# Turned squares with the place in the quarter outermost, and their copies three steps later

## The chip, the cores and the metric

The kernel runs on one core of a Trainium2 chip. The metric is the time of the whole kernel on the device in microseconds (us); lower is better. Times before and after are medians of several runs; a profile is one further execution that the hardware profiler recorded.

## What is computed

Two layers follow one another. The first is a gated attention without softmax: the scores of a sequence with itself are symmetric, the negative ones are cut off, and the rest is squared. The second sends each of the 19,968 resulting rows through one of eight small networks, chosen by a hash of its token.

```python
B, S, D = 8, 2496, 256          # z has 64 columns
scores = (1.0 / S) * np.matmul(z, z.transpose(0, 2, 1))
attn = np.maximum(scores, 0.0) ** 2
x = (u * np.matmul(attn, v)).reshape(B * S, D)

expert_idx = token_ids * np.int64(2654435761) % 8
for e in range(8):              # w1: 256 x 1024, w2: 1024 x 256
    mask = expert_idx == e
    out[mask] = np.maximum(x[mask] @ w1[e], 0.0) @ w2[e]
```

All values are 32-bit floats.

## The kernel before

**Tiles and groups.** A sequence has 2496 positions: 19 tiles of 128 and one of 64 (tile number `TM` = 19). Four tiles make a group, so a batch has `NG` = 5 groups g = 0 to 4; the last has 448 positions, the others 512. The kernel goes through the 8 batches b, and in each through its groups: `for n, (b, g) in enumerate(groups)`. A group's positions are the queries, columns of the matmuls. For each group it sums, over all 20 tiles t of keys, `v[t]` times the squared scores of tile t with the group. The sum stands in two PSUM tiles `acc`, one for each half of the 256 columns of v.

**Half of the scores are never computed.** As scores are symmetric, `scores(b, g)` (line 203) computes only the key tiles from the group's own on; these squares are called fresh and lie in tiles `made[b, g, key group]`, 128 partitions by 4 key tiles by 512 queries, from the pool `apool` of six rooms. TensorE writes a score tile to PSUM (line 210, six buffers, `mm_ps`), ScalarE writes its ReLU to the room (line 218; for g = 0 VectorE takes every eighth, line 216), and later ScalarE squares it in place (line 226). What lies on the other side of the diagonal is obtained by turning: a room of 4 by 4 tiles is transposed into a `mirror` tile, which a later group reads. Seven mirror tiles exist (one serves the routing's sorting at first, `sorting`, and in the expert stage their room holds weights).

**How a room is turned.** VectorE's transpose works on squares of 32 by 32. `turns_of` (line 234) does a room in four turns c, one for each quarter of 32 columns: VectorE transposes the quarter's squares into a buffer `stage` of 128 partitions by 512 elements (line 241, pool `spool`, five buffers). The four quarters r of the stage's partitions must then go to partitions c of the mirror: three of them by DMA from SBUF to SBUF, issued by SyncE (line 251), and the fourth, which stays on its partitions, by a copy on ScalarE (line 249). The mirror's layout is (partition, i, r, s, q): query tile i, place r of the query in its tile's quarters, key tile s, and q in the quarter. So a row of 512 elements of the stage is broken into four pieces of 128 elements (512 bytes), or three where the last group's fourth tile has no such quarter. Rooms on the diagonal are completed in place by small transposes on VectorE (`own_turns`, line 262).

**The order of the work** is written out by hand (`order = tc.manual_schedule()`, line 569): each engine's instructions stand in its queue as the program emits them, and an engine takes them in that order. A step of the attend loop (lines 664 to 691) emits two matmuls, the halves of one key tile (`attend`, line 319), then two squares, then turns, 1.2 a step on average (`turn_scores`, line 280), then `between` (line 595), which counts the steps in `i` and also places the routing's small work. `turn_scores` first emits the copies of the turns of the step before (`to_copy`). `turn_now` forces what a reader still lacks. At a step of t = 8 the group's u is loaded (`load_u`); for g = 1, 2, 3, 4 parts of the next batch's v are loaded too, at g = 3 the next batch's z. All of these, like the mirrors' transfers, are issued by SyncE. After the loop `attend_last` (line 326) takes the half tile 19, then the next group's scores are emitted, then the last three key tiles (`LATE`), half after half, each followed by `gate`.

**Leaving the group.** `gate` (line 334) transposes acc on VectorE into `x_q` (line 339, pool `qpool`, two buffers), writes it to DRAM (`x_way`, four DMAs, line 346) so that quarters and columns change places, and three steps later reads it back as rows (`fetch`, lines 349 and 351, one DMA or, for the last group, two). GpSimd multiplies by u and places each row at the slot of its expert. The columns of acc stand in the order of the queries: tile i outside, then r, then q. `squares` (line 308) gives the matmul its columns: fresh squares are contiguous there, mirrors are read in runs of 32.

From about 1560 us on the second layer runs: for blocks of rows of one expert, two chains of matmuls (lines 742 and 754).

Of the kernel before, what the change touches and what calls it, by code (L numbers as in the profile page):

```python
# [10 lines left out]
F32 = mybir.dt.float32  # L11
# [13 lines left out]
def kernel(  # L25
# [10 lines left out]
    nc = tc.nc  # L36

    B, S, D = u.shape
    K = z.shape[-1]
    N = B * S  # L40
    E, _, F = moe_w1.shape
# [15 lines left out]
    NQ = P // Q  # L57
# [11 lines left out]
    def pool(name, bufs, **kw):  # L69
        return ctx.enter_context(tc.tile_pool(name=name, bufs=bufs, **kw))  # L70
# [8 lines left out]
    NA = NG + 1  # L79
    apool = pool("apool", NA)  # L80
    xpool = pool("xpool", 3)
    qpool = pool("qpool", 2)
    spool = pool("spool", 5)

    x_dram = nc.dram_tensor("x_rows", (NS * P, D), F32)

    x_way = [nc.dram_tensor(f"x_way_{k}", (G, NQ, Q, D), F32) for k in range(2)]


    slot_dram = nc.dram_tensor("slot_tokens", (P * NS,), I32)
# [30 lines left out]
    zn, zT, v_sb, u_sb, x_q, made, mirror, to_square, to_turn, to_fetch, gated = {}, {}, {}, {}, {}, {}, {}, [], [], [], []  # L123
# [110 lines left out]
    def turns_of(b, a, g):  # L234

        key = b, a, g
        def turn(c):
            if key not in mirror:
                mirror[key] = mirrors.pop(0)
            stage = spool.tile([P, G * G * Q], F32, name="stage")  # L240
            nc.vector.transpose(stage[:].rearrange("p (n q) -> p n q", q=Q),  # L241
                                made[key][:].rearrange("p t (s q) -> p (t s) q", q=P)[:, :, ts(c, Q)])
            for r in range(NQ):

                m = len(group(g)) if r * Q < width(group(g)[-1]) else G - 1
                o = mirror[key][ts(c, Q), 0:m, r].rearrange("p i s q -> p i (s q)")
                x = stage[ts(r, Q), 0:m * G * Q].rearrange("p (i n) -> p i n", i=m)
                if r == c:
                    to_copy.append((key, lambda o=o, x=x: nc.scalar.copy(o, x)))  # L249
                else:  # L250
                    nc.sync.dma_start(o, x)
        for c in range(NQ):
            yield lambda c=c: turn(c)

# [22 lines left out]
    to_copy = []  # L277
    share = 0

    def turn_scores(steps):  # L280

        nonlocal share
        copy_turned(to_copy[:])
        share += 1.2 * steps
        own = [e for e in to_turn if e[0][1] == e[0][2]][:3]
        others = [e for e in to_turn if e[0][1] < e[0][2]]
        for e in own:
            turn(e)
        while share >= 1 and others and (mirrors or others[0][0] in mirror):
            turn(others.pop(0))  # L290
            share -= 1
        share = min(share, 1)

    def turn(e):
        to_turn.remove(e)
        e[1]()

    def copy_turned(those):
        for e in those:
            to_copy.remove(e)  # L300
            e[1]()

    def turn_now(key):
        for e in [e for e in to_turn if e[0] == key]:
            turn(e)
        copy_turned([e for e in to_copy if e[0] == key])

    def squares(b, g, t):

        if t in fresh(b, g):  # L310
            a = made[b, g, t // G][:, t % G, :].rearrange("p (n q) -> p n q", q=Q)
        else:
            a = mirror[b, t // G, g][:].rearrange("p i r s q -> p s (i r) q")[:, t % G]
        return a[:, 0:queries(g) // Q]

# [3 lines left out]
    def attend(b, g, k, acc, halves):  # L319
        t = summed(b, g)[k]  # L320
        turn_now((b, t // G, g))
        for h in halves:
            nc.tensor.matmul(acc[h][:, 0:queries(g)], v_sb[b][:, t, h::2], squares(b, g, t),  # L323
                             start=(k == 0), stop=(k == TM - 1), skip_group_check=True)

    def attend_last(b, g, acc):

        turn_now((b, TM // G, g))
        for h in range(2):
            rows = ds(h * R, R)  # L330
            nc.tensor.matmul(acc[h][:, 0:queries(g)], v_sb[b][rows, TM, h::2], squares(b, g, TM)[rows],
                             start=False, stop=False, skip_group_check=True)

    def gate(b, g, h, acc):
        n = queries(g) // Q
        if h == 0:
            x_q[b, g] = qpool.tile([P, G * NQ, D // NQ], F32, name="x_q")
        x = x_q[b, g]
        nc.vector.transpose(x[:, 0:n, h::2], acc[h][:, 0:n * Q].rearrange("p (n q) -> p n q", q=Q))  # L339
        if h == 0:  # L340
            return

        xs = xpool.tile([P, G, D], F32, name="x_sb")
        o = x_way[g % len(x_way)]
        for a in range(NQ):
            nc.sync.dma_start(o[:].rearrange("i j p d -> p (i j) d")[:, 0:n, ts(a, D // NQ)], x[ts(a, Q), 0:n])
# [38 lines left out]
    def places():  # L385

        with tc.tile_pool(name="route", bufs=1) as route:
# [20 lines left out]
            room = sorting[:].rearrange("p i r s q -> p (i r s q)")  # L408
# [21 lines left out]
            for e in range(0, E, H):  # L430
                m = min(H, E - e)
# [17 lines left out]
            first, count, whole, upto_w, before_w, rest, parts, upto_p, thr, start, jump, late = (  # L449
                per_e[:, k, :] for k in range(12))  # L450
# [163 lines left out]
    w1, w2, xg, xT, hT, w_buf, xg_buf, xT_buf = {}, {}, {}, {}, {}, [], [], []  # L614
# [12 lines left out]
                x_dram[ds(c * P, n * P), ts(r, D // NQ)].rearrange("(k i) d -> i k d", i=Q))  # L627

    def load_w(j, k):
        w1[j] = w_buf[2 * k][:].rearrange("p i r s q -> p (i r s q)").rearrange("p (h f) -> p h f", h=DP)  # L630
        w2[j] = w_buf[2 * k + 1][:].rearrange("p i r s q -> p (i r s q)").rearrange("p (c d) -> p c d", c=FP)
# [15 lines left out]
    mirrors = [mpool.tile([P, G, NQ, G, Q], F32, name=f"m_{k}") for k in range(NG * NG // 4)]  # L647

    sorting = mirrors.pop()
    scores(0, 0)  # L650
    for n, (b, g) in enumerate(groups):
# [5 lines left out]
        acc = [acc_ps.tile([P, G * P], F32, name="acc", tag="acc") for _ in range(2)]  # L657
# [39 lines left out]
        if n + 1 < len(groups):  # L697

            m = len(fresh(*groups[n + 1])) // G
# [15 lines left out]
    for _, f in to_fetch:  # L715
        f()
    while gated:
        place_x()

# [130 lines left out]
```

## Time and profile before

| | us |
|---|---|
| median of 3 runs | 2682.76 |
| lowest and highest run | 2680.69, 2684.29 |
| the profiled execution | 2685.0 |
| its span, first to last instruction | 2683.3 |
| mean granted clock of TensorE in it | 0.996 |
| VectorE waits for stage buffers (`m<-stage` DMA) | 179.5 |
| ScalarE's copy waits for VectorE's stage | 139.7 |
| SyncE issues a mirror transfer, median | 0.599 |

PE is TensorE's matmuls, PEld its weight loads (beside the matmuls), DVE is VectorE, ACT ScalarE, POOL GpSimd, SP SyncE; "SPq" rows are the DMAs that SyncE issues, and their length is the time of issuing, not of the transfer. A row of groups reads: line, engine, operation, what it writes and reads, shape, count, then busy time in us and the mean of one in ns, then the idle time just before these instructions and who ended it. A row of waits: who waited for whom, us in total, times, the longest. A row of the timeline: start, length, engine, line, count, and in brackets the idle time before it. In tables of stretches: stretch, length, busy time, granted clock, the share of time in which the DMA engines were busy, and GB/s.

TensorE's busy time is 2652.4 us of the span; the chain of waits that ended last is made almost only of TensorE's own matmuls. The DMA engines are busy for half the time in the attention, at some 100 to 155 GB/s in the page's slices.

### The profile page before, as it was taken

The numbers are of one execution on the slowest core, as the hardware profiler recorded it, in microseconds if no ns is written. First come the engines' busy times: TensorE is split into PE (matmuls) and PEld (weight loads), VectorE is DVE, ScalarE is ACT, GpSimd is POOL, SyncE is SP. The second block draws the span as 40 slices with busy tenths as digits, with TensorE's granted clock in tenths as the row PEclk, the third lists the DMA queues.
The fourth block names the chain that finished last, engine by engine and source line by source line (L and its number), as shares of the span: only waits on it lengthen the run. The fifth ranks groups of instructions, "written<-read, shape, count | busy, mean of one in ns | idle before, by whom it ended". The sixth has DMA issues, their size and how long they took to land. (4 is left out here: it accounts for less than half of the span.)

```text
span 2683.3 us, 28098 instructions
## 1 busy us (share of the span) xinstructions
PE 2652.4 (99%) x8854; PEld 1534.3 (57%) x8854; DVE 795.7 (30%) x2147; ACT 785.0 (29%) x1592; POOL 608.9 (23%) x671
## 2 busy tenths in 40 slices
PE   9999999999999999999999999999999999999999
PEld 5444444444444444444444457777777777777777
DVE  5634334434334333344344311111111111111110
ACT  7316326324334345245245101111111111111111
POOL 1331332233233233232321121111111111111112
PEclk9999999999999999999999999999999999999999
DMA  5544445545435534534534386666666666666663
GB/s 150 155 119 99 117 109 115 116 105 121 113 99 129 111 102 112 121 98 114 131 97 115 92 204 160 159 158 157 155 154 161 163 164 163 163 164 161 159 156 87
DMA packets 524247, 357.21 MB, mean 133 GB/s; under 512 B 277660, under 2 KB 487085, under 8 KB 524096
## 3 DMA queue, kind: packets, MB, share of 16 engines
q1 hardware_dynamic: 503360, 314.29, 50.1%
q0 software_dynamic: 20736, 41.09, 4.8%
q8 instruction: 72, 1.18, 0.2%
q14 instruction: 79, 0.65, 0.1%
HBM read 229.36 MB, written 67.53 MB: 111 GB/s over the span
## 5 line engine op out<-in xcount | busy, mean ns | idle before, releaser
L323 PE MATMUL acc<-a,v_sb 128*128 128x512 f32 (+1 forms) x1760 | 768.0, 593 | 0.0
L742 PE MATMUL h_ps<-v_sb,m 128*128 128x128 f32 (+1 forms) x2080 | 569.6, 432 | 3.0 <-DVE v_sb L644 1.9
L323 PEld LDWEIGHTS acc<-a,v_sb 128*128 128x128 f32 x1760 | 343.0, 197 | 391.6 <-issue 374.7
L754 PE MATMUL o_ps<-m,hT 128*128 128x256 f32 x2576 | 566.3, 379 | 0.0
L323 PE MATMUL acc<-m,v_sb 128*128 128x512 f32 (+1 forms) x1280 | 529.2, 571 | 5.5 <-DVE x_q L339 4.5
L754 PEld LDWEIGHTS o_ps<-m,hT 128*128 128x128 f32 x2576 | 487.0, 190 | 78.3 <-issue 15.0
L742 PEld LDWEIGHTS h_ps<-v_sb,m 128*128 128x128 f32 x2080 | 318.1, 191 | 238.0 <-issue 231.4
L323 PEld LDWEIGHTS acc<-m,v_sb 128*128 128x128 f32 x1280 | 250.5, 196 | 279.8 <-issue 267.7
L748 DVE TENSOR_SCALAR hT<-h_ps 128x512 f32<-128x512 f32 x161 | 111.4, 692 | 946.3 <-PE h_ps L742 540.6
L218 ACT ACTIVATE a<-s_ps 128x512 f32<-128x512 f32 (+3 forms) x456 | 203.6, 566 | 588.5 <-PE s_ps L210 439.6
L766 POOL DMA_INDIRECT out_dram<-o_sb,idx x157 | 153.6, 979 | 925.0 <-ACT o_sb L761 917.1
L354 POOL TENSOR_TENSOR x_sb<-x_sb,u_sb 128x256 f32<-128x256 f32 (+1 forms) x160 | 111.1, 723 | 989.0 <-DMA x_sb<-x_way 766.1
L262 DVE STREAM_TRANSPOSE a<-a 32x64 f32<-32x64 f32 (+3 forms) x1408 | 298.8, 241 | 20.0 <-ACT a L226 6.4
L249 ACT COPY m<-stage 32x512 f32<-32x512 f32 (+1 forms) x320 | 189.6, 593 | 300.9 <-DVE stage L241 139.7
L241 DVE STREAM_TRANSPOSE stage<-a 128x512 f32<-128x512 f32 x320 | 218.0, 700 | 200.8 <-DMA m<-stage 179.5
L226 ACT ACTIVATE a<-a 128x512 f32<-128x512 f32 (+1 forms) x480 | 236.9, 564 | 2.1
L761 ACT COPY o_sb<-o_ps 128x256 f32<-128x256 f32 x161 | 60.0, 372 | 596.6 <-PE o_ps L754 596.6
L210 PE MATMUL s_ps<-zT 64*128 64x512 f32 (+2 forms) x960 | 207.6, 555 | 16.7 <-ACT a L218 11.3
L339 DVE STREAM_TRANSPOSE x_q<-acc 128x512 f32<-128x512 f32 (+1 forms) x80 | 56.4, 705 | 552.1 <-PE acc L323 501.5
L746 ACT ACTIVATE hT<-h_ps 128x512 f32<-128x512 f32 x161 | 96.1, 597 | 398.9 <-PE h_ps L742 390.7
L210 PEld LDWEIGHTS s_ps<-zT 64*128 64x128 f32 x960 | 118.4, 192 | 123.0 <-issue 75.6
L562 POOL DMA_INDIRECT x_rows<-x_sb,slot_i x160 | 157.7, 986 | 43.2 <-issue 37.2
(93 smaller groups left out, 390.2 us busy)
## 6 DMA issues: line engine op xcount, KB each, us to landing
m<-in_moe_w_dram SPq DMA_DIRECT2D x260, 256.0 KB
m<-in_moe_w_dram SPq DMA_DIRECT2D x65, 1024.0 KB
m<-stage SPq DMA_DIRECT2D x768, 64.0 KB
v_sb<-in_v_dram SPq DMA_DIRECT2D x32, 512.0 KB
u_sb<-in_u_dram SPq DMA_DIRECT2D x32, 512.0 KB
x_way<-x_q SPq DMA_DIRECT2D x128, 128.0 KB
x_sb<-x_way SPq DMA_DIRECT2D x32, 512.0 KB
v_sb<-x_rows SPq DMA_DIRECT2D x128, 128.0 KB
```

The source lines that it names most:

```text
L210: nc.tensor.matmul(ps[:, lo:n], zT[b][h, ts(t, P)], zT[b][h, ds(g * G * P + lo, n - lo)], start=True, stop=True)
L218: nc.scalar.activation(a, ps[:, lo:n], AF.Relu)
L226: nc.scalar.activation(a, a, AF.Square, scale=1.0 / S)
L241: nc.vector.transpose(stage[:].rearrange("p (n q) -> p n q", q=Q), made[key][:].rearrange("p t (s q) -> p (t s) q", q=P)[:, :, ts(c, Q)])
L249: to_copy.append((key, lambda o=o, x=x: nc.scalar.copy(o, x)))
L262: return lambda: nc.vector.transpose(out, in_)
L323: nc.tensor.matmul(acc[h][:, 0:queries(g)], v_sb[b][:, t, h::2], squares(b, g, t), start=(k == 0), stop=(k == TM - 1), skip_group_check=True)
L562: st = nc.gpsimd.indirect_dma_start(out=x_dram[:, :], out_offset=bass.IndirectOffsetOnAxis(ap=slot_i[0:width(c % T), c:c + 1], axis=0), in ...
L742: nc.tensor.matmul(ps[:, ts(i, n)], w1[j][:, c, ts(k * m + i, P)], xT[j][:, :, c, :], start=(c == 0), stop=(c == DP - 1))
L748: nc.vector.tensor_scalar_max(o, ps[:], 0.0)
L754: nc.tensor.matmul(ps[:], hT[j][f][:, ts(t, P)], w2[j][:, f, :], start=(f == 0), stop=(f == FP - 1))
L766: st = nc.gpsimd.indirect_dma_start(out=out[:], out_offset=bass.IndirectOffsetOnAxis(ap=rows, axis=0), in_=o, in_offset=None, bounds_check ...
```

## The change

The mirror's layout becomes (partition, r, i, s, q): the place in the quarter goes outermost. A turn's transfer and its copy are then one row of 512 elements (2 KB) on either side for each of 32 partitions. For the last group's queries the full row is moved, also where the fourth tile has no quarter. The columns of acc now stand in the order r, i, q for all; so fresh squares are read in that order too, in runs of 32. In the last group the quarters r = 0 and 1 have four tiles and r = 2 and 3 have three, so `squares` gives two parts, of 256 and 192 columns, and each matmul there becomes two, with one start of the accumulation. The way back of x is read by four DMAs, one for each r. ScalarE's copy of the quarter that stays is no longer emitted with the next step's turns: it goes to the list `to_fetch` with the step i + 3, and `between` emits what is due. One `x_q` buffer is given up and one stage buffer gained.

```diff
-    qpool = pool("qpool", 2)
-    spool = pool("spool", 5)
+    qpool = pool("qpool", 1)
+    spool = pool("spool", 6)
...
-    x_way = [nc.dram_tensor(f"x_way_{k}", (G, NQ, Q, D), F32) for k in range(2)]
+    x_way = [nc.dram_tensor(f"x_way_{k}", (G * NQ, Q, D), F32) for k in range(2)]
...
             for r in range(NQ):
-                m = len(group(g)) if r * Q < width(group(g)[-1]) else G - 1
-                o = mirror[key][ts(c, Q), 0:m, r].rearrange("p i s q -> p i (s q)")
-                x = stage[ts(r, Q), 0:m * G * Q].rearrange("p (i n) -> p i n", i=m)
-                if r == c:
-                    to_copy.append((key, lambda o=o, x=x: nc.scalar.copy(o, x)))
-                else:
-                    nc.sync.dma_start(o, x)
+                o, x = mirror[key][ts(c, Q), r].rearrange("p i s q -> p (i s q)"), stage[ts(r, Q)]
+                if r != c:
+                    nc.sync.dma_start(o, x)
+                else:
+                    to_fetch.append((i + 3, key, lambda o=o, x=x: nc.scalar.copy(o, x)))
...
-        copy_turned(to_copy[:])
         share += 1.2 * steps
...
-    def copy_turned(those):
-        for e in those:
-            to_copy.remove(e)
-            e[1]()
+    def fetch(due):
+        for e in [e for e in to_fetch if due(e)]:
+            to_fetch.remove(e)
+            e[2]()
...
         if t in fresh(b, g):
-            a = made[b, g, t // G][:, t % G, :].rearrange("p (n q) -> p n q", q=Q)
+            a = made[b, g, t // G][:, t % G, :].rearrange("p (i r q) -> p r i q", r=NQ, q=Q)
         else:
-            a = mirror[b, t // G, g][:].rearrange("p i r s q -> p s (i r) q")[:, t % G]
-        return a[:, 0:queries(g) // Q]
+            a = mirror[b, t // G, g][:, :, :, t % G, :]
+        parts, c = [], 0
+        for r in ([slice(0, NQ)] if TM not in group(g) else [slice(0, R // Q), slice(R // Q, NQ)]):
+            m = G if r.start < R // Q else G - 1
+            n = (r.stop - r.start) * m * Q
+            parts.append((slice(c, c + n), a[:, r, 0:m]))
+            c += n
+        return parts
...
         for h in halves:
-            nc.tensor.matmul(acc[h][:, 0:queries(g)], v_sb[b][:, t, h::2], squares(b, g, t),
-                             start=(k == 0), stop=(k == TM - 1), skip_group_check=True)
+            for cols, a in squares(b, g, t):
+                nc.tensor.matmul(acc[h][:, cols], v_sb[b][:, t, h::2], a,
+                                 start=(k == 0 and cols.start == 0), stop=(k == TM - 1), skip_group_check=True)
...
-        m = len(whole(g))
-        def fetch():
-            nc.sync.dma_start(xs[:, 0:m], o[0:m].rearrange("i j p d -> (j p) i d"))
-            if m < G:
-                nc.sync.dma_start(xs[0:R, m], o[m, 0:R // Q].rearrange("j p d -> (j p) d"))
+        def rows_of_x():
+            c = 0
+            for r in range(NQ):
+                m = G if r * Q < width(group(g)[-1]) else G - 1
+                nc.sync.dma_start(xs[ts(r, Q), 0:m], o[c:c + m].rearrange("i p d -> p i d"))
+                c += m
...
-        to_fetch.append((i + 3, fetch))
+        to_fetch.append((i + 3, None, rows_of_x))
...
     def between():
-        if to_fetch and to_fetch[0][0] <= i:
-            to_fetch.pop(0)[1]()
+        fetch(lambda e: e[0] <= i)
```

`attend_last` gets the same two parts in the last group, with the halves inside the loop over parts. `turn_now` emits a forced turn's copy by `fetch(lambda e: e[1] == key)`. The names of the layout's dimensions change where the mirrors' room is used for the sorting and for the weights.

More of the change, by code (lines that the diff above doesn't have):

```diff
@@ L275, in own_turns @@
                         yield move(tiles[ds(h * R + c * Q, Q), 3, 0:3, ts(r, Q)], tiles[i, 0:3, 3, ts(c, Q)])
-    to_copy = []
     share = 0
@@ L305, in turn_now @@
             turn(e)
-        copy_turned([e for e in to_copy if e[0] == key])
+        fetch(lambda e: e[1] == key)
     def squares(b, g, t):
         if t in fresh(b, g):
-            a = made[b, g, t // G][:, t % G, :].rearrange("p (n q) -> p n q", q=Q)
+            a = made[b, g, t // G][:, t % G, :].rearrange("p (i r q) -> p r i q", r=NQ, q=Q)
         else:
-            a = mirror[b, t // G, g][:].rearrange("p i r s q -> p s (i r) q")[:, t % G]
-        return a[:, 0:queries(g) // Q]
+            a = mirror[b, t // G, g][:, :, :, t % G, :]
[6 more added lines that the diff above has]
+        return parts
     def attend(b, g, k, acc, halves):
@@ L322, in attend @@
         for h in halves:
-            nc.tensor.matmul(acc[h][:, 0:queries(g)], v_sb[b][:, t, h::2], squares(b, g, t),
-                             start=(k == 0), stop=(k == TM - 1), skip_group_check=True)
+            for cols, a in squares(b, g, t):
+                nc.tensor.matmul(acc[h][:, cols], v_sb[b][:, t, h::2], a,
+                                 start=(k == 0 and cols.start == 0), stop=(k == TM - 1), skip_group_check=True)
     def attend_last(b, g, acc):
         turn_now((b, TM // G, g))
[L329 to L332, printed above, removed]
+        for cols, a in squares(b, g, TM):
+            for h in range(2):
+                rows = ds(h * R, R)
+                nc.tensor.matmul(acc[h][:, cols], v_sb[b][rows, TM, h::2], a[rows],
+                                 start=False, stop=False, skip_group_check=True)
     def gate(b, g, h, acc):
@@ L345, in gate @@
         for a in range(NQ):
-            nc.sync.dma_start(o[:].rearrange("i j p d -> p (i j) d")[:, 0:n, ts(a, D // NQ)], x[ts(a, Q), 0:n])
-        m = len(whole(g))
-        def fetch():
-            nc.sync.dma_start(xs[:, 0:m], o[0:m].rearrange("i j p d -> (j p) i d"))
-            if m < G:
-                nc.sync.dma_start(xs[0:R, m], o[m, 0:R // Q].rearrange("j p d -> (j p) d"))
+            nc.sync.dma_start(o[:].rearrange("n p d -> p n d")[:, 0:n, ts(a, D // NQ)], x[ts(a, Q), 0:n])
+        def rows_of_x():
[4 more added lines that the diff above has]
+                c += m
             for k, t in enumerate(group(g)):
@@ L407, in places @@
             total, rank = counts[:, 0], counts[:, 1]
-            room = sorting[:].rearrange("p i r s q -> p (i r s q)")
+            room = sorting[:].rearrange("p r i s q -> p (r i s q)")
             upto = room[:, 0:E * C].rearrange("p (e c) -> p e c", e=E)
@@ L629, in load_w @@
     def load_w(j, k):
-        w1[j] = w_buf[2 * k][:].rearrange("p i r s q -> p (i r s q)").rearrange("p (h f) -> p h f", h=DP)
-        w2[j] = w_buf[2 * k + 1][:].rearrange("p i r s q -> p (i r s q)").rearrange("p (c d) -> p c d", c=FP)
+        w1[j] = w_buf[2 * k][:].rearrange("p r i s q -> p (r i s q)").rearrange("p (h f) -> p h f", h=DP)
+        w2[j] = w_buf[2 * k + 1][:].rearrange("p r i s q -> p (r i s q)").rearrange("p (c d) -> p c d", c=FP)
         e = nc.sync.value_load(eb_i[0:1, j:j + 1], min_val=0, max_val=E - 1)
@@ L646 @@
     mpool = pool("mirror", 1)
-    mirrors = [mpool.tile([P, G, NQ, G, Q], F32, name=f"m_{k}") for k in range(NG * NG // 4)]
+    mirrors = [mpool.tile([P, NQ, G, G, Q], F32, name=f"m_{k}") for k in range(NG * NG // 4)]
     sorting = mirrors.pop()
@@ L714 @@
     assert not to_turn and next(place, None) is None and i > SORT + 4 * C
-    for _, f in to_fetch:
-        f()
+    fetch(lambda e: True)
     while gated:
```

## The prediction

> **What bounds the kernel now.** I read the page's busy times first, then the groups kept apart by shape, the waits, TensorE's busy time in stretches of 10 us, and last the timeline around one hole. From the page and the groups by shape:
>
> ```profile
> PE 2652.4 (99%) x8854; PEld 1534.3 (57%) x8854; DVE 795.7 (30%) x2147; ACT 785.0 (29%) x1592; POOL 608.9 (23%) x671
> L323 PE MATMUL acc<-a,v_sb 128*128 128x512 f32 x1664 | 730.9, 596 | 0.0
> L754 PE MATMUL o_ps<-m,hT 128*128 128x256 f32 x2576 | 566.3, 379 | 0.0
> L323 PE MATMUL acc<-m,v_sb 128*128 128x512 f32 x768 | 333.5, 592 | 0.0
> L323 PE MATMUL acc<-m,v_sb 128*128 128x448 f32 x512 | 195.7, 541 | 5.5 <-DVE x_q L339 4.5 <-issue 1.0
> L742 PE MATMUL h_ps<-v_sb,m 128*128 128x128 f32 x1056 | 123.2, 275 | 0.0
> L323 PE MATMUL acc<-a,v_sb 128*128 128x448 f32 x96 | 38.3, 548 | 0.0
> ```
>
> TensorE is the bound: 99% busy, so time saved elsewhere counts only if it closes a hole in TensorE. Records overlap, so the price of one is busy time over count, not the mean: 512 columns 730.9/1664 = 0.439 us for fresh squares `a` and 333.5/768 = 0.434 for mirrors `m`; 448 columns 234.0/608 = 0.385 (both rows together); 256 columns 0.220; 128 columns 0.117. (An f32 matmul leaves two records.)
>
> In stretches of 10 us TensorE is full except at some group changes. From g=0 to g=1 of batches 1 to 6 I add up 11.4 us idle (240 to 250 us is one: 7.95 busy), from g=1 to g=2 5.0 us, at the start of g=4 5.5 us. The first and the last batch have no hole from g=0 to g=1. SyncE's queue and then all engines at the hole of batch 1:
>
> ```profile
> 222.59 13.73 SPq L251 DMA_DIRECT2D m<-stage  x21
> 236.41 0.53 SPq L120 DMA_DIRECT2D u_sb<-in_u_dram  x1
> ...
> 237.12 1.14 PE L331 MATMUL acc<-a,v_sb 64*128 64x512 f32 x4
> 238.09 2.74 PE L210 MATMUL s_ps<-zT 64*128 64x512 f32 x12
> 242.23 1.57 ACT L218 ACTIVATE a<-s_ps 128x512 f32<-128x512 f32 x3 [5.02 <-PE s_ps L210]
> 242.88 1.71 PE L210 MATMUL s_ps<-zT 64*128 64x512 f32 x2 [2.05 <-ACT a L218]
> ```
>
> Six score tiles fill the six PSUM buffers from 238.09 on; ScalarE, idle, empties the first only at 242.23, some 3 us after it was written; TensorE stands 2.05 us. What is odd just then is the load of u, 512 KB, issued at 236.41. Its place in the program is t=8, eight attend steps of 4 x 0.43 = 1.7 us before the change: some 13 us late. In batch 0 the same load goes out at 41.27 and its change starts at 46.8: no hole. I take the late burst as what delays the hand-over from TensorE to ScalarE; the records show the coincidence, not the cause. The load is late because SyncE is solid with mirror transfers: 21 in 13.73 us, 0.65 us each, and VectorE and ScalarE wait in the same ring:
>
> ```profile
> DVE stage L241 <- DMA m<-stage: 179.5, 109, 4.0
> ACT m L249 <- DVE stage L241: 139.7, 88, 4.8
> PEld s_ps L210 <- ACT a L218: 37.3, 82, 3.2
> PE s_ps L210 <- ACT a L218: 11.3, 8, 2.4
> ```
>
> After five holes the clock falls as well:
>
> ```profile
> 243.00:246.00 3.00, 3.00 (x7) 0.50 0.39 82
> ```
>
> The stretches of 10 us below full clock lose 10.2 us of work in all.
>
> **What the Trainium skill says.** Perfetto Trace Analysis, "What 'DMA-bound' means": a sequencer solid with DMA slices is busy making descriptors, not moving data, and large descriptors are what help; this is SyncE from 209 to 237 us. TensorE: Matmul & The Clock Gate, "What's actually happening": after an idle window the array runs at half clock for windows of about 3.4 us; the trace agrees (0.50 from 243 to 246 us). Same page, "Back-to-back issue gap": a fixed cost of about 2.5 ns for each matmul besides its columns; the prices above give 2 to 10 ns. SBUF — State Buffer, "Door 1": reads pay for crossing into new 16-byte lines; runs of 32 f32 fill theirs, and mirrors, read in such runs, cost 0.434 against 0.439 us contiguous.
>
> **The change part by part.** *Mirror transfers.* 960 stay (12 for each turned square), each now 32 rows of 2 KB in place of 128 (or 96) pieces of 512 B; the 192 short ones grow from 48 to 64 KB, 3.1 MB more of 357. Issue takes 0.599 us now (median). The new form is not in the trace. Nearest rows: 0.39 us (the 1 MB weight load L636), 0.53 (u, above), so 0.35 to 0.60; I take 0.45. Up to the load of u a g=0 has 36 of them from 209.1 to 236.4 us: at 0.50 with the gap instead of 0.65 that is 5.4 us, less 0.8 for the longer x load below, and u leaves at about 231.8, 5.3 us before the change, as in batch 0. *TensorE, what comes free:* the holes from g=0 and g=1, 11.4 + 5.0, the clock 10.2, and some 2 us hidden under the modelled ends of matmuls: 28.6. The holes at g=4 (after the z load, which stays) I leave. I take five sixths: -24 us. Below: 0.
> *The split in g=4.* 19 x 2 + 2 = 40 instructions a batch become 80: 640 records of 448 columns become as many of 256 and of 192. Between 128 and 256 columns a line gives 0.168 for 192: 0.220 + 0.168 - 0.385 = +0.003 us, 640 times: +2 us. Upper bound: if the second weight load (0.196 us a record) isn't hidden behind 192 columns, +0.028 x 640 = +18 us. Against that, 1056 records of 128 columns, each with its own weights, ran at 0.117.
> *Fresh squares read in runs of 32:* 0, by the mirrors' row; up to +0.01 us x 1760 = +18 if three dimensions cost something that two don't. Below nothing is excluded: contiguous already.
> *ScalarE's copies, three steps later:* none is added; 64 grow from 384 to 512 columns, 64 x (614 - 507 ns) = 6.8 us on an engine that is 29% busy. They no longer hold squares behind VectorE (139.7 us of waits), but TensorE hardly waits for squares: 0. The built order puts no copy between a group's ReLUs, so the scores have none in front that weren't there. A stage is held three steps longer; the sixth buffer covers 1.2 turns x 4 steps = 4.8. If it didn't, VectorE stalls and, behind it, the transposes of acc (L339) that free PSUM.
> *x:* one `x_q` instead of two: the next group's transpose waits for stores issued a group (some 37 us) earlier: 0. The load of x is four DMAs in place of one or two, +112 on SyncE at about 0.4 us over the whole attention, 0.8 to 1.2 us a group: in the sum above, otherwise off the path.
> *The expert stage* (from 1560 us) keeps its instructions; only the rearrangement of the same 16 KB is renamed: 0.
>
> Sum: -24 + 2 = -22 on the profiled execution of 2685.0 us (span 2683.3), so 2663; the median of the runs shown is 2.2 lower. 2662, rounded.
>
> **Rivals.** *A, nothing moves (0.18):* SyncE's issue stays near 0.6 us, or the holes don't come from the load. For it: 0.6 is the same for pieces of 4 x 512 and 3 x 512, so it doesn't follow the descriptor count. Against: forms with four times the descriptors (x stores) take 0.51. Holes stay, the split adds 2: 2684. The issue must fall below about 0.53 for u to gain 3 us, so this is also where a half gain starts.
> *B, slower (0.12):* the second weight load shows. Place: every 192-column record in g=4; price 18 us. It decides if weights take their 0.196 us apart from the matmul before; then 2683 + 18 = 2701 with the holes left. With the holes closed it would be 2677, still faster, so it needs A's first half too. Against: the 128-column row.
> *C, slower (0.11):* a stage isn't free in time. VectorE then waits for ScalarE's late copies, PSUM is freed late at group changes: 0.7 us (the hole at g=4) x 32 changes = +22: 2705. For: VectorE already waits 179.5 us for stages. Against: two steps' slack by the count above.
>
> **How the numbers follow.** Forecast 0.59, A 0.18, B 0.12, C 0.11. The forecast's own range is 2650 (all 28.6, and the g=4 holes) to 2675 (a third of the gain). A measurement can tell 0.2%, 5.4 us, from no change. Faster: the forecast, 0.59. Same: A, 0.18. Slower: 0.23. To leave no more than 2 in 10 out, the range runs from 2648 past A to the lower half of B and C: 2695.
>
> **What would show it.** Right: SyncE's L251 near 0.45 us; u issued more than 4 us before each change; TensorE full at 240, 435 and 630 us; fewer half-clock windows; waits of VectorE for `m<-stage` well below 179.5; 192-column records at about 0.165. Wrong: L251 still at 0.6, or u early and the holes still there (then the load isn't the cause), or the fresh squares above 0.445 us.

## The result and the profile after

| | before | after |
|---|---|---|
| median of 20 runs each, us | 2680.91 | 2673.36 |
| lowest and highest run, us | 2674.82, 2684.29 | 2668.14, 2680.16 |
| the profiled execution, us | 2685.0 | 2668.14 |
| SyncE issues a mirror transfer, median us | 0.599 | 0.588 |

The ratio of after to before is 0.9976, with a 95% interval from 0.9968 to 0.9984: 7.5 us faster, a third of the 21 us that were forecast (2682.76 less 2662). The two profiled executions differ by 16.9 us, more than the medians: that of before is above the highest of its 20 runs, that of after is its lowest. So the traces are compared place by place and not by their totals.

First TensorE's busy time and its matmuls by shape in the trace of after:

```profile
PE 2644.8 (99%) x9494; PEld 1633.1 (61%) x9494; DVE 796.1 (30%) x2147; ACT 789.0 (30%) x1592; POOL 608.2 (23%) x671
...
L327 PE MATMUL acc<-a,v_sb 128*128 128x512 f32 x1664 | 728.8, 594 | 0.0
L327 PE MATMUL acc<-m,v_sb 128*128 128x512 f32 x768 | 333.5, 592 | 0.0
...
L327 PE MATMUL acc<-m,v_sb 128*128 128x256 f32 x512 | 152.5, 379 | 0.3 <-DVE x_q L344 0.3
L327 PE MATMUL acc<-m,v_sb 128*128 128x192 f32 x512 | 125.1, 326 | 0.0
```

Fresh squares, now read in runs of 32, take 728.8/1664 = 0.438 us a record, against 0.439 before. The rows of 256 and 192 columns overlap each other in time, so their busy times can't be added; all of L327 together is busy 766.1 + 529.0 = 1295.1 us, against 768.0 + 529.2 before. The 1280 additional weight loads show in PEld's total (1633.1 against 1534.3) and in no wait of TensorE.

Then SyncE, TensorE and ScalarE at the hole of batch 1, the place shown before, in the timeline of after:

```profile
221.45 13.76 SPq L246 DMA_DIRECT2D m<-stage  x21
...
235.79 2.74 PE L210 MATMUL s_ps<-zT 64*128 64x512 f32 x12
235.91 0.70 SPq L120 DMA_DIRECT2D u_sb<-in_u_dram  x1
...
239.67 7.30 ACT L218 ACTIVATE a<-s_ps 128x512 f32<-128x512 f32 x16 [5.75 <-PE s_ps L210]
240.32 4.89 PE L210 MATMUL s_ps<-zT 64*128 64x512 f32 x20 [1.79 <-ACT a L218]
```

What the forecast rests on hasn't happened here. Again 21 transfers take 13.8 us, the load of u leaves 0.1 us after the first score matmul (before: 1.7 us ahead of it), and ScalarE again starts some 3 us late: TensorE stands 1.79 us, against 2.05.

TensorE in stretches of 10 us of after (stretch, length, busy time, granted clock, DMA share, GB/s):

```profile
230.00:240.00 10.00, 8.53 (x28) 1.00 0.55 145
240.00:250.00 10.00, 9.68 (x32) 1.00 0.28 66
280.00:290.00 10.00, 9.70 (x31) 1.00 0.28 100
430.00:440.00 10.00, 8.51 (x33) 1.00 0.46 127
...
940.00:950.00 10.00, 9.70 (x51) 1.00 0.61 134
```

The holes are still at the same changes, and smaller: added up as before, 8.9 us from g=0 to g=1 (11.4 before), 2.6 from g=1 to g=2 (5.0), 0.3 at the start of g=4 (5.5). In this execution no stretch of the attention fell below full clock after a hole. But this is the fastest of 20 runs: in e5 below, the same kernel in an execution near its median, the three sums are 10.3, 4.5 and 3.4 us.

The waits in the ring of the stages, in the same form as before:

```profile
ACT m L248 <- DVE stage L241: 112.4, 62, 4.4
DVE stage L241 <- DMA m<-stage: 106.9, 88, 3.6
...
PEld s_ps L210 <- ACT a L218: 34.1, 88, 2.7
PE s_ps L210 <- ACT a L218: 9.2, 7, 1.8
```

VectorE's wait for stages fell from 179.5 to 106.9 us; TensorE's waits for ScalarE hardly moved (37.3 and 11.3 before). What the shorter wait of VectorE paid can't be read here. Where there are no holes, e4 and e13 below, with the later copies and the sixth buffer, differ from before by less than can be told from no change.

### The profile page after: what moved, and what is told of

Read it like the earlier page. It is cut to its first block, busy times and chain, and to the rows that moved or that the text cites. A ratio compares the mean times of both kernels' runs of the same rounds, so it can differ in the third digit from the quotient of the medians.

```text
span 2666.4 us, 29585 instructions
## 1 busy us (share of the span) xinstructions
PE 2644.8 (99%) x9494; PEld 1633.1 (61%) x9494; DVE 796.1 (30%) x2147; ACT 789.0 (30%) x1592; POOL 608.2 (23%) x671
## 5 line engine op out<-in xcount | busy, mean ns | idle before, releaser
L327 PE MATMUL acc<-a,v_sb 128*128 128x512 f32 (+2 forms) x1856 | 766.1, 570 | 0.0
L327 PEld LDWEIGHTS acc<-a,v_sb 128*128 128x128 f32 x1856 | 357.5, 196 | 374.6 <-issue 357.0
L327 PE MATMUL acc<-m,v_sb 128*128 128x512 f32 (+2 forms) x1792 | 529.0, 455 | 0.3 <-DVE x_q L344 0.3
L327 PEld LDWEIGHTS acc<-m,v_sb 128*128 128x128 f32 x1792 | 335.1, 196 | 193.2 <-issue 180.8
L248 ACT COPY m<-stage 32x512 f32<-32x512 f32 x320 | 196.5, 614 | 257.6 <-DVE stage L241 112.4
L241 DVE STREAM_TRANSPOSE stage<-a 128x512 f32<-128x512 f32 x320 | 215.4, 696 | 145.0 <-DMA m<-stage 106.9
```

Of the source, the lines that this page charges most:

```text
L248: to_fetch.append((i + 3, key, lambda o=o, x=x: nc.scalar.copy(o, x)))
L327: nc.tensor.matmul(acc[h][:, cols], v_sb[b][:, t, h::2], a, start=(k == 0 and cols.start == 0), stop=(k == TM - 1), skip_group_check=True)
```

## The experiments

Several kernels were run beside the kernel before on the same chip; the chips differed between the groups, and this became the main finding. Ratios are to the kernel before on the same chip, with the 95% interval.

**Load u, and v, earlier.** If the late burst of u makes the holes, moving the load is the direct test.

```diff
-            if t == 8:
+            if t == 2:
                 load_u(b, g)
...
-    V_LOADS = [(4, 4), (1, 9), (2, 9), (3, 6), (3, 12)]
+    V_LOADS = [(4, 4), (1, 4), (2, 4), (3, 4), (3, 8)]
```

e1 has the first part of this on the kernel after, e2 both.

> The kernel after, with the group's u loaded at t = 2 of its attend loop in place of t = 8; nothing else. Theory (the late u burst makes the holes from g=0 to g=1): u leaves some 10 us before the change, the 8.9 us that TensorE is idle there in batches 1 to 6 of the kernel after go, the time is about 2664.5 us (2673.4 - 8.9), ratio to before 0.994; the smaller holes from g=1 to g=2 stay, as the load of v still goes out there. Rival 1 (the holes come from the mirror transfers themselves, or from GpSimd's small indirect writes, which stay): the holes stay at 0.9 us or more per change though u is early, the time is about 2673, ratio 0.9976. Rival 2 (u merely moves the burst): the holes stay away at the change but appear in the middle of the group's loop; there nothing is handed over that TensorE needs within microseconds, so this is told from the theory only by idle at other places.

> As e1, and the loads of the next batch's v at g=1 and g=2 at t = 4 in place of 9, at g=3 at t = 4 and 8 in place of 6 and 12. Theory (any 512 KB burst from HBM at a group change makes the hole): besides the 8.9 us from g=0 to g=1 the 2.6 us from g=1 to g=2 go, time about 2662, ratio 0.993. Rival 1 (the loads are not the cause): as the kernel after, 2673, ratio 0.9976. If only u matters, e2 equals e1.

**Divide the change.** e3 is the layout alone, e4 the later copies alone, on the layout of before.

```diff
 e3, from after
-    qpool = pool("qpool", 1)
-    spool = pool("spool", 6)
+    qpool = pool("qpool", 2)
+    spool = pool("spool", 5)
...
-                    to_fetch.append((i + 3, key, lambda o=o, x=x: nc.scalar.copy(o, x)))
+                    to_fetch.append((i + 1, key, lambda o=o, x=x: nc.scalar.copy(o, x)))
 e4, from before
-    qpool = pool("qpool", 2)
-    spool = pool("spool", 5)
+    qpool = pool("qpool", 1)
+    spool = pool("spool", 6)
...
-                    to_copy.append((key, lambda o=o, x=x: nc.scalar.copy(o, x)))
+                    to_copy.append((i + 3, key, lambda o=o, x=x: nc.scalar.copy(o, x)))
...
-        copy_turned(to_copy[:])
...
+        copy_turned([e for e in to_copy if e[0] <= i])
```

> The new layout alone: the kernel after with the copies emitted with the next step (i + 1), two x_q buffers and five stage buffers, as before. Theory A (the 7.5 us gained come from the layout: fewer and longer pieces to move): as the kernel after, about 2673, ratio 0.9976. Theory B (they come from the copies three steps later and the sixth stage buffer, which take the waits from ScalarE and VectorE): as before or worse by the split of g=4, 2681 to 2683, ratio 1.000 to 1.001.

> The late copies alone: the kernel before, its layout kept, with the copies three steps later, one x_q buffer and six stage buffers. Theory A (the layout brings the gain): as before, 2681, ratio 1.000. Theory B (the later copies and the sixth buffer bring it): about 2673, ratio 0.997. Half each would be 2677 in e3 and in e4.

Measured, on one chip: before 2638.45 us; e1 2639.93 (1.0004, 0.9996 to 1.0013), e2 2640.07 (1.0004, 0.9995 to 1.0012), e3 2639.81 (1.0004, 0.9995 to 1.0012), e4 2637.22 (0.9996, 0.9988 to 1.0004). The kernel before itself took 42 us less than where the change had been measured, and no expectation fits. The timeline of e3 at the change of batch 1 says why:

```profile
220.50 13.19 SPq L246 DMA_DIRECT2D m<-stage  x21
...
233.66 1.14 PE L336 MATMUL acc<-a,v_sb 64*128 64x512 f32 x4
233.79 0.53 SPq L120 DMA_DIRECT2D u_sb<-in_u_dram  x1
...
234.56 0.98 POOL L556 DMA_INDIRECT slot_tokens<-token,addr  x1 [0.31 <-issue]
234.64 6.60 PE L210 MATMUL s_ps<-zT 64*128 64x512 f32 x32
235.69 7.31 ACT L218 ACTIVATE a<-s_ps 128x512 f32<-128x512 f32 x16 [0.63 <-PE s_ps L210]
```

The same 21 transfers without a pause, the same u just as late (0.85 us ahead of the scores): yet ScalarE starts 1.05 us after the first score matmul, not 3.9, and 32 score matmuls run in one piece of 6.60 us. Stretches of 10 us of e3 where after has its holes:

```profile
230.00:240.00 10.00, 10.00 (x39) 1.00 0.63 165
280.00:290.00 10.00, 10.00 (x25) 1.00 0.29 52
430.00:440.00 10.00, 10.00 (x24) 1.00 0.38 77
```

So a late load of u isn't enough for a hole, and on this chip there are no holes for the change to close. The issue of a mirror transfer can be compared here too, in the rows of the line that issues it, first e3, then e4 (shortest, median and longest in ns):

```profile
L246 SPq DMA_DIRECT2D m<-stage x960: 507/588/1842, 19.4 to 1464.4; - x192
```

```profile
L251 SPq DMA_DIRECT2D m<-stage x960: 585/599/1748, 19.7 to 1463.1; - x192
```

11 ns for a quarter of the pieces, on both chips.

**The kernel after once more (e5), and e2 once more (e6).** They tell a property of the chip from one of the kernels.

> The kernel after, unchanged. In the first four runs the kernel before took 2638.45 us, where it had taken 2680.91 when the change was measured, and TensorE had no hole in any of them, although e3 issues u as late as the kernel after does. Theory C (the holes belong to the chip that a kernel runs on: there the completions that engines report to each other come late by microseconds): where the kernel before takes about 2638 us, after takes 2638 to 2641 us, ratio 1.000 to 1.001, TensorE full at all group changes; where before takes about 2681 us, after takes about 2673, ratio 0.9976, and the holes are there. Theory D (the holes belong to the kernels, and e1 to e4 all happened to remove them): after takes 0.2% less than before also where before takes 2638 us, or has holes there.

> The kernel after with u at t = 2 and the loads of v at t = 4 and 8, as in e2. Where the kernel before takes about 2638 us: as e2, 2640 us, ratio 1.0004. Where it takes about 2681 us: if the burst of u and v sets off the late hand-overs, the holes at the group changes go and the time is about 2662 (2673.4 less 8.9 and 2.6), ratio 0.993; if it does not, 2673, ratio 0.9976.

They ran on another chip, and there the holes are: before 2686.75 us, e5 2682.44 (0.9982, 0.9974 to 0.9991), e6 2696.87 (1.0037, 1.0025 to 1.0050). The main part of theory C holds: e6 is the very kernel that took 2640.07 as e2, 57 us more on this chip. (That completions come late there is its proposal, which no run measures.) And the load theory falls: with u and v early the kernel is 14 us slower than e5, for a reason that isn't known. The timeline of e6 at batch 1:

```profile
225.45 0.37 SPq L120 DMA_DIRECT2D u_sb<-in_u_dram  x1
...
239.40 0.98 POOL L556 DMA_INDIRECT slot_tokens<-token,addr  x1 [0.30 <-issue]
239.45 2.74 PE L210 MATMUL s_ps<-zT 64*128 64x512 f32 x12
240.68 0.98 POOL L556 DMA_INDIRECT slot_tokens<-token,addr  x1 [0.30 <-issue]
244.27 7.31 ACT L218 ACTIVATE a<-s_ps 128x512 f32<-128x512 f32 x16 [5.39 <-remote]
244.92 4.89 PE L210 MATMUL s_ps<-zT 64*128 64x512 f32 x20 [2.73 <-ACT a L218]
```

u is out 14 us ahead, far more than the forecast had hoped for, and the hole is larger: ScalarE starts 4.8 us after the first score matmul and TensorE stands 2.73 us. The stretches of e6 that answer to those of after:

```profile
240.00:250.00 10.00, 7.27 (x33) 1.00 0.30 71
280.00:290.00 10.00, 8.02 (x27) 1.00 0.35 90
1230.00:1240.00 10.00, 9.23 (x25) 0.66 0.25 59
```

**What goes out at the changes that have holes.** I went through the 156 changes of the four traces with holes (before, after, e5, e6), counted a hole where TensorE stands over 0.5 us in the 8 us from the first score matmul on, and asked whether GpSimd issues one of its 160 slot writes (`enter`, 4 bytes a row into `slot_tokens`, L556, L550 in before) between 0.5 us ahead of that matmul and 6 us after. With such a write: 24 of 24 changes to g=1, 17 of 24 to g=2, 2 of 2 to g=3, 5 of 28 to g=4 and 0 of 1 to g=0 have a hole. Without one: 0 of 77. (At g=4 only four key tiles are left, for six PSUM buffers; there TensorE stands later, where it needs acc again: in 16 of the 28 within 14 us.)

Idle time shows only a part of what is lost. The time from the first score matmul to the attend matmul that follows the scores shows more. At the change to g=1 of batch 1 that matmul stands in before, after and e3 at

```profile
248.68 1.56 PE L323 MATMUL acc<-a,v_sb 128*128 128x512 f32 x3
...
245.15 5.42 PE L327 MATMUL acc<-a,v_sb 128*128 128x512 f32 x12
...
241.16 5.42 PE L327 MATMUL acc<-a,v_sb 128*128 128x512 f32 x12
```

which is 10.6, 9.4 and 6.5 us after the first score matmul. In all batches of e3 it is 6.5 us to g=1 and 4.6 to g=2; in the four traces with holes all 48 changes to g=1 and g=2 with a slot write take at least 1.1 us longer. Over batches 1 to 6 that adds up to 35.0 us in before (against 16.4 us of idle time, 11.4 and 5.0), 25.9 in after, 33.6 in e5 and 46.6 in e6. Of the 77 changes without a slot write four take over 0.5 us longer, 0.6 to 0.9 us: three to g=0, whose last slot write went out 0.7 to 1.0 us ahead of the scores, and the one to g=1 in batch 0 of before, which is as late in e9 below, on a chip without holes.

Batch 7 of after is one of the changes without: SyncE does what it does in batch 1 (21 transfers, u, 12 transfers), the load is about as late, but the slot writes are all done, and there is no hole. (The loads of the next batch are missing there too, but in batch 1 SyncE issues none of them near this change either.)

```profile
1377.66 13.23 SPq L246 DMA_DIRECT2D m<-stage  x21
1390.98 0.53 SPq L120 DMA_DIRECT2D u_sb<-in_u_dram  x1
1391.62 7.47 SPq L246 DMA_DIRECT2D m<-stage  x12
1391.70 6.60 PE L210 MATMUL s_ps<-zT 64*128 64x512 f32 x32
1392.76 7.30 ACT L218 ACTIVATE a<-s_ps 128x512 f32<-128x512 f32 x16 [2.49 <-PE s_ps L210]
```

The slot writes begin near the change to g=3 of batch 0 and end near that to g=4 of batch 6; this would fit the first and the last batch having no holes from g=0 to g=1. In batch 1 GpSimd waits for x until late in the group and then catches up with nine indirect writes in a row, four of x and five of slots, which end at the change. But it is a coincidence in traces, and the writes aren't enough for a hole either: in e3 they go out at the change as well. To show a cause, the writes must be taken away or moved, on a chip with holes. e7 leaves them out of the kernel after; e8 makes five at a time, e9 does so in the kernel before (the lines that count `entered` are left out here).

```diff
 e7
-            enter((i - SORT) // 4)
+            if (i - SORT) // 4 == C - 1:
+                nc.gpsimd.dma_start(idx[:], slot_dram[:].rearrange("(p c) -> p c", p=P))
 e8, e9
-        elif i % 4 == 0 and i < SORT + 4 * C:
-            assert next(place, None) is None
-            enter((i - SORT) // 4)
+        elif i % 21 == 0 and entered < C:
+            assert next(place, None) is None
+            for _ in range(5):
+                enter(entered)
+                entered += 1
```

> The kernel after without the 160 indirect writes of slot_tokens by GpSimd (L556), so no row of the output is stored in the expert stage either (every slot holds the number of no token). Where before takes about 2685 us (holes): theory G (GpSimd's run of indirect writes, which catches up on its wait for x and ends at each change from batch 1 to 6, is what delays the hand-overs): the holes at the changes go, the attention ends some 30 us earlier, about 2650 us, ratio 0.987. Theory M (the mirror transfers and loads alone do it): holes as in e5, ratio 0.998. Where before takes about 2638 us no theory expects a hole: ratio 1.000.

> The kernel after with the slot writes moved: five at the first step of a group in place of one every four steps. GpSimd makes them before it waits for x, so its run after x has come is four indirect writes, not eight or nine, and ends some 5 us before the change. Where before takes about 2685 us: theory G: most of the holes from g=0 to g=1 go, about 2655 to 2665 us, ratio 0.988 to 0.992. Theory M: as e5, 2682, ratio 0.998. Theory G2 (any small indirect write delays hand-overs, wherever it stands): the same number of writes, ratio 0.998, but holes at other places, at the start of groups. Where before takes about 2638 us: ratio 1.000 to 1.001.

> The kernel before with the slot writes moved as in e8. Where before takes about 2685 us: theory G: as e8 or 1 to 2 us better, for want of the split in g=4: ratio 0.988 to 0.992; that would be the whole of the gain that the change was forecast to bring, without the change. Theory M: ratio 1.000. Where before takes about 2638 us: ratio 1.000.

These fell on the first experiments' chip: before 2638.81; e7 2639.66 (1.0001, 0.9993 to 1.0010), e8 2639.90 (1.0002, 0.9993 to 1.0010), e9 2638.95 (0.9999, 0.9990 to 1.0007). Without holes nothing is told of their cause. (A group has 20 steps, not 21, so in e8 and e9 the five writes wander through the groups; the expectations say the first step.) The kernels of e7, e8, e3 and e4 were run again as e10 to e13:

> The kernel of e7 once more (no slot writes, so no row of the output is stored). Where before takes about 2685 us: theory G (GpSimd's run of indirect writes at the changes makes the holes): about 2650 us, ratio 0.987. Theory M (mirror transfers and loads alone): as the kernel after, 2682, ratio 0.998. Where before takes about 2638 us: ratio 1.000, and nothing is told.

> The kernel of e8 once more. Where before takes about 2685 us: theory G: 2655 to 2665 us, ratio 0.988 to 0.992. Theory M: ratio 0.998. Theory G2 (each small indirect write delays hand-overs, wherever it stands): ratio 0.998 with holes at the start of groups. Where before takes about 2638 us: ratio 1.000.

> The kernel of e3 once more: the layout without the later copies and with five stage buffers. Where before takes about 2685 us: theory A (the layout brings the gain): 0.998; theory B (the later copies and the sixth stage buffer bring it): 1.000 to 1.001. Where before takes about 2638 us: 1.0004 as in e3.

> The kernel of e4 once more: the layout of before with the later copies, one x_q and six stage buffers. Where before takes about 2685 us: theory A: 1.000; theory B: 0.997 to 0.998. Where before takes about 2638 us: 0.9996 as in e4.

A third chip, and again none: before 2638.90; e10 2638.13 (1.0000, 0.9991 to 1.0008), e11 2640.35 (1.0002, 0.9994 to 1.0011), e12 2639.77 (1.0001, 0.9993 to 1.0010), e13 2637.33 (0.9994, 0.9986 to 1.0002). e12 and e13 repeat e3 and e4 within 0.2 us.

Then the variants were put into different batches of one kernel, so that a single execution compares them: e14 on the kernel after, e15 on e4 (shown is e14; the step that takes `slots_due()` in place of one write is left out).

```diff
+    def slots_due():
+        if b == 2:
+            return 0
+        if b in (3, 4):
+            return 5 if i % 20 == 0 else 0
+        return 1 if i % 4 == 0 else 0
...
-                    to_fetch.append((i + 3, key, lambda o=o, x=x: nc.scalar.copy(o, x)))
+                    to_fetch.append((i + (1 if b == 5 else 3), key, lambda o=o, x=x: nc.scalar.copy(o, x)))
```

> The kernel after with the variants batch by batch: batches 1 and 6 as in after; batch 2 without slot writes; batches 3 and 4 with five slot writes at the first step of a group (20 steps) in place of one in four steps; batch 5 as after but the copies with the next step; batch 7 with slot writes one in four steps, where after has none left. Read by the idle time of TensorE at the change from g=0 to g=1. Where before takes about 2685 us: theory G (GpSimd's run of indirect slot writes up to the change makes the hole): about 1.5 us idle in batches 1, 5, 6 and 7, none in batch 2, at most a third in 3 and 4. Theory M (mirror transfers and loads): 1.5 us in all of 1 to 6, and none in 7. If the later copies are what makes the holes smaller, batch 5 has some 2 us. Where before takes about 2638 us: no holes in any.

> The same mix on the kernel of e4 (the layout of before, six stage buffers, copies three steps later, in batch 5 with the next step). Where before takes about 2685 us: if the layout makes the holes smaller, batches 1 and 6 have about 2 us idle from g=0 to g=1 as in before, against 1.5 in e14; if the later copies do, they have 1.5 and batch 5 has 2. Theories G and M as in e14. Where before takes about 2638 us: no holes in any.

One execution each, on a fourth chip: before 2639.54, e14 2639.92, e15 2636.76, no hole in any batch. e14's kernel was run three more times (e16, e17, e18), with what is in substance one expectation:

> The kernel of e14 once more, read by the idle time of TensorE at the change from g=0 to g=1 of each batch. Where before takes about 2685 us: theory G: about 1.5 us in batches 1, 5, 6 and 7, none in batch 2, at most a third in 3 and 4. Theory M: 1.5 us in all of 1 to 6, none in 7. If the later copies make the holes smaller, batch 5 has some 2 us. Where before takes about 2638 us: no holes in any.

Before 2638.73, 2638.83 and 2640.93; the kernel 2640.60, 2638.50 and 2638.83; the first two on a fifth chip, the last again on the third, no hole in any. So no variant without or with moved slot writes ever met a chip with holes, and the cause of the holes stays open.

## Why the prediction was wrong

Point by point, in the prediction's own steps.

**The issue of a mirror transfer, "I take 0.45 us": the first step that failed.** It is 0.588, from 0.599, so SyncE stays solid and u leaves no earlier. The sign against it stood in the prediction, under rival A: 0.6 was the price for four pieces and for three. I let the skill's advice on large descriptors (Perfetto Trace Analysis, "What 'DMA-bound' means") outweigh that row. Another page limits it: DMA: Bandwidth & Descriptors, "Why small descriptors are slow (HBM only)", says that transfers from SBUF to SBUF don't pay the penalty of small ones. It speaks of moving the data, which no run here measures by itself; that the issue doesn't follow the pieces either is what the 11 ns of these rows show.

**"I take the late burst as what delays the hand-over": the second step that failed, and the graver.** Even with u early the gain wouldn't have come: e6 issues u 14 us ahead and has larger holes, and batch 7 of after has the late burst, in a trace with holes, and has none. (e3 has the burst and no hole too, but on a chip where nothing makes one.) What delays the hand-over in its place stays open. The text said that the records show the coincidence and not the cause, and then gave five sixths of the holes to it. A second coincidence, the slot writes, fits batches 0 and 7 as well and could have been read in GpSimd's timeline of before: there they run until 239.89 us, while ScalarE waits for its first score tile.

**The sum, -24 us for holes and clock.** The size of the holes wasn't overrated: 28.6 us were counted, with 2 us for what idle time doesn't show, and the changes to g=1 and g=2 alone took 35.0 us longer than in e3, a part of it at reduced clock. What failed is that five sixths of it would go. The holes belong to the chip as much as to the kernel. Where they are, the change gained 7.5 us (0.9976) and 4.3 us (e5 beside before, 0.9982); where they are not, every complete kernel with the new layout (e1, e2, e3, e8, e11, e12) lies between 1.0001 and 1.0004, within what can be told from no change; the kernel after itself was not run there. The 7.5 us thus seem to come out of holes that shrank. That agrees with the stretches, which lost 10 us of idle time between the two traces, half of it at g=4, where the prediction put nothing. But a single execution is a weak witness: e5, the same kernel as after, has nearly the holes of before (33.6 us against 35.0) and again shows stretches at reduced clock.

```profile
240.00:250.00 10.00, 8.15 (x25) 0.83 0.30 72
480.00:490.00 10.00, 9.55 (x24) 0.83 0.00 0
1210.00:1220.00 10.00, 7.21 (x27) 0.83 0.47 120
```

Which part of the change shrank the holes isn't known: e3, e4, e12 and e13 all ran where there are none. One thing that moved with them, again in these two traces: the last slot write near a change to g=1 goes out 0.4 us after the first score matmul on average in after, 1.2 us in before (batches 1 to 6); to g=2 it is 1.6 against 2.2.

**The split of g=4, +2 us; the second weight load hidden.** Right. Where there are no holes the mirrors' matmuls of g=4 in batch 7 can be compared directly, first e3 (split) with the matmul that follows, then e4 (not split):

```profile
1484.74 24.38 PE L327 MATMUL acc<-m,v_sb 128*128 128x256 f32 x128
1509.05 1.04 PE L336 MATMUL acc<-a,v_sb 64*128 64x256 f32 x8
...
1483.72 24.22 PE L322 MATMUL acc<-m,v_sb 128*128 128x448 f32 x64
1507.87 1.03 PE L330 MATMUL acc<-a,v_sb 64*128 64x448 f32 x4
```

From start to start that is 24.31 us against 24.15. From the start of one record to the next a part of 256 columns takes 0.216 us and one of 192 takes 0.163 (medians in e3), together 0.379 against 0.376 for 448 in e4: 0.003 us, 640 times, are the 2 us. The sum was right though the prices weren't quite: busy time over count gave 0.220 and 0.385, and the fixed cost of a record that was read out of them, 2 to 10 ns, can't be got from them; from start to start two records of 256 columns take 3 ns more than one of 512 (0.429). The medians agree: e3 and e12 are 1.4 and 0.9 us above before and 2.6 and 2.4 above e4 and e13, though each interval includes no change. Rival B, 18 us, is out.

**Fresh squares in runs of 32, at 0:** right, 0.438 against 0.439 us. **The copies three steps later, at 0:** not contradicted where there are no holes (e1 and e2, which have them, took 0.1 to 0.3 us more than e3, which has not); where there are, open. **One x_q buffer, at 0:** not contradicted; TensorE's wait for x_q was 4.5 us in before, 0.3 in after and 3.4 in e5. **x in four DMAs:** 1.90 us of SyncE in place of 0.98 at batch 1, so 0.92 more, inside the 0.8 to 1.2 that was put in.

**The rivals and the signs.** A was right in its first half (issue near 0.6) and nearer in time than the forecast (2684 and 2662, against 2673), and still missed: it had the holes as fixed. C didn't come: VectorE waits less for stages, not more. Two signs of being wrong came, L251 still at 0.6 and, in e6, u early with the holes still there. One sign of being right came too, VectorE's shorter wait for stages, but the mechanism it was to stand for did not. That 2673 lies inside the range that was given is luck.

## What to carry to other kernels

A hole that always stands beside a transfer is not yet made by it: look for a place that has the transfer and no hole (here batch 7), and count every queue's traffic at both before putting a price on it. When the same kernel may meet different chips, ask what a change is worth on one where the hole doesn't exist; here that is nothing that could be told from no change. A price that is the same for three pieces and for four is a warning that it may not follow the pieces at all: here it fell by 11 ns for one.

## What the runs showed of the hardware

**Chips differ.** The same kernel before took 2638.5 to 2640.9 us on four chips (medians or, on two of them, single executions) and 2686.75 (2680.94 to 2699.25) on another, 1.8% more, though the issue times above and the attend matmuls by shape are the same (728.7 us for the 1664 records of 512 columns in e3, 729.4 in e5). The loss lies in the attention: the second layer starts at 1556.9 us in e5 and at 1514.7 in e3, the layout alone, which is 42 of the 44 us between their spans, and e3 has no hole there. Three of the chips without holes were met twice, the one with holes once; whether the first measurement (2680.91) ran on it isn't on record. So that it is the chip, and not the host or the hour, is likely and not shown. A single chip would have shown these holes as the kernel's own.

**A hand-over can take microseconds though the engine that receives is idle.** The skill says that a matmul's end in a trace is computed, and that the next engine sees it only once PSUM has acknowledged the write and the semaphore update has travelled (Perfetto Trace Analysis, "Tensor Engine Instruction (MATMUL, LD_WEIGHTS)"). In e3 this whole way, from the start of the first score matmul to ScalarE's start, takes 1.05 us; in after 3.9 and in e6 4.8 at the same place, with the six PSUM buffers then full. VectorE is late in the same way: its first transpose of acc at g=4 starts 3.9 us after the first score matmul in all batches of e3, and up to 7.0 us after it in e5. None of the runs says what holds it up.

**The price of issuing a transfer from SBUF to SBUF** on SyncE was 0.588 us (median) for 32 rows of 2 KB and 0.599 us as pieces of 512 B, both where there are holes (after and before) and where there are none (e3 and e4).
